# Attention written as a list of 260 operations that overlaps three batches, and the first output weights prepared during the experts

## The chip, the cores and the metric

The kernel runs on one core of one Trainium2 chip. The metric is the device time of one execution, in microseconds (us). Before the change three runs took 483.46, 483.88 and 485.32 us; the median is 483.88 us. The names of the engines are those of the profile: PE is TensorE, DVE is VectorE, ACT is ScalarE, POOL is GpSimd and SP is SyncE, which issues the transfers here.

## The reference, cut to what matters

Three layers follow each other: an attention between 512 tokens and 32 state rows of each head (8 batches, 8 heads, 64 columns), a soft mixture of 8 experts over all 4608 rows, and a gated layer over the same rows.

```python
scores = x @ state.T * scale;  a = softmax(scores);   xread = a @ state      # per batch and head
scores2 = state @ x.T * scale; a2 = softmax(scores2); sread = a2 @ x
x = concat([xread, sread])                            # rows: 8 * (512 + 32), 512 columns
logits = x @ phi                                      # 32 slots
d = softmax(logits, over all rows); slot_input = d.T @ x
slot_out[e] = relu(slot_input[e] @ w1[e]) @ w2[e]     # 8 experts, 4 slots each
y = softmax(logits, over slots) @ slot_out
g = y @ w_gate;  out = (g * sigmoid(g) * (y @ w_val)) @ w_out
```

## The kernel before

All instructions are recorded in the order of the Python text, and every engine works through its own part of that order, one instruction after the other. Nothing reorders them; an instruction that waits holds up everything behind it on its engine.

The attention takes one batch per turn of `for b in range(B - 1)`. A turn computes the scores of batch b (`scores`: PE matmuls into a PSUM bank pair, ACT copy into the one SBUF tile `stsA`), the largest score of each state row (`scores_max`, DVE), the shift of `stsA` by it (`state_shift`, DVE), transposes of the unshifted scores (`tr8`, PE) with the row maxima and the subtraction (`attn_sub`, DVE), the exponentials (`attn_exp`, ACT), the row sums and reciprocals (`attn_norm`, DVE) and the multiplication (POOL). In the same turn the state side is done (`state_tr`, `sread_mm`, `sread_out`), and the logits and slot sums of the two batches before (`attn_tr`, `logits_mm`, `logits_max`, `logits_exp`, `logits_tr`, `slots_mm`, `slots_out`). `load_T` makes the transposed x of batches 3 to 7 on PE. The last batch stands behind the loop, cut into two halves of 256 tokens, with `fill` matmuls that compute nothing used. Behind it come the 64 state rows' own logits (`sr_T`, `sr_mm`, `sr_exp`, `sr_tr`), the weights of the batches among each other (`mx`, `gm`, `w`, `Jw`), and the slot inputs `siT`.

Large PSUM tiles come from three bank pairs in turn (`pbig`), small ones from two banks in turn (`psmall`), so a PE group also waits for whoever reads the tile that had the bank before it.

All loads stand in one list and are issued by SP in that order (`pump`). A tile of the weight ring (17 tiles of 1 MB) or one of the borrowed attention tiles (`A`, `a2`, `e2`, `a0`, `at`) takes the next weights when the attention has finished with it.

The experts come in two groups of four: `expert_1` (w1), `expert_r` (relu), `expert_h` (transposes), `expert_2` (w2), `expert_o` (slot outputs to `ST`). Between them stand pieces of other work: the softmax over slots (`c_calc`), the first gate and value weights (`prep_w0`), and the first output weights. The output weights arrive as float64 bits and are rebuilt as float32 by `to32` (one ACT and three DVE instructions). Of the first 1 MB of them one half is loaded early and rebuilt by `prep_wo0`; the other half comes behind the last expert weights, and `wo0_load`, `wo0_shift`, `wo0_bits`, `wo0_scale`, `wo0_hi` and `wo0_lo` rebuild, scale and split it. Their instructions stand inside `expert_o(1)`, `prep_first` and the start of the main loop. `prep_first` goes from the slot outputs to the first gate and value weights; then the main loop (`front`, `middle`, `back`) runs over the rows.

Of the kernel before, what the change touches and what calls it, by code (L numbers as in the profile page):

```python
# [66 lines left out]
def attn_moe_glu_kernel(  # L67
# [152 lines left out]
    def load_T(b, half):  # L220
        if b >= B or b not in XT_PE:
            return
# [6 lines left out]
        p = pbig([128, 2, S])  # L229
        for kk in range(2):  # L230
            kc = 2 * half + kk
            for j in range(4):
                pe.transpose(p[:, kk, j * 128:(j + 1) * 128], x_[:, j, kc, 1:129], ident)
        (act.copy, XTE)[half](out=xT[b][:, 2 * half:2 * half + 2, :], in_=p)  # L234

    def score_mm(b, x_, p, cols):
        n = cols.stop - cols.start
        for pr in range(4):
            for hh in range(2):
                r = slice(64 * hh, 64 * hh + 64)  # L240
                pe.matmul(out=p[32 * pr:32 * pr + 32, hh, 0:n], lhsT=stB[r, b, pr, :], rhs=x_[r, pr, cols],
                          start=True, stop=True)

    def scores(b):
        x_ = xT.pop(b) if b in XT_PE else got.pop(("xt", b))
        p = pbig([128, 2, S])
        score_mm(b, x_, p, slice(0, S))
        done()
        t = stsA
        act.activation(out=t, in_=p, func=AF.Copy, scale=SCALE)  # L250
        sts[b] = t

    def scores_max(b):
        nm = sm.tile([128, 2], F32, tag="nm2", name="nm2")
        dve.tensor_reduce(out=nm, in_=sts[b], axis=AX.X, op=ALU.max, negate=True)  # L255
        RZ[b] = nm

    def state_shift(b):
        nm, t = RZ.pop(b), sts[b]
        for q in range(2):  # L260
            dve.tensor_scalar(out=t[:, q, :], in0=t[:, q, :], scalar1=nm[:, q:q + 1], scalar2=None, op0=ALU.add)  # L261

    def tr8(src):
        p = pbig([128, 4, 256])
        for j in range(4):
            for q in range(2):
                pe.transpose(p[:, j, q * 128:(q + 1) * 128], src[q][:, j * 128:(j + 1) * 128], ident)  # L267
        return p

    def attn_sub(b):  # L270
        t = sts[b]
        v = tr8([t[:, 0, :], t[:, 1, :]])
        state_shift(b)
        a = wk.tile([128, 4, 256], F32, tag=f"a{b % 3}", name="a")
        for i in range(2):
            vi, ai = (u[:, 2 * i:2 * i + 2, :].rearrange("p j (h s) -> p (j h) s", s=NS) for u in (v, a))
            m1 = sm.tile([128, 16], F32, tag="m1", name="m1")
            dve.tensor_reduce(out=m1, in_=vi, axis=AX.X, op=ALU.max)  # L278
            dve.tensor_tensor(out=ai, in0=vi, in1=bc(m1, NS), op=ALU.subtract)  # L279
        A[b] = a  # L280

    def attn_exp(b):
        a = A[b]
        for i in range(2):
            act.activation(out=a[:, 2 * i:2 * i + 2, :], in_=a[:, 2 * i:2 * i + 2, :], func=AF.Exp)  # L285

    def attn_norm(b):
        a = A[b]
        av = a.rearrange("p j (h s) -> p (j h) s", s=NS)
        z = sm.tile([128, 32], F32, tag="z", bufs=1, name="z")  # L290
        for i in range(2):
            dve.tensor_reduce(out=z[:, 16 * i:16 * i + 16], in_=av[:, 16 * i:16 * i + 16, :], axis=AX.X, op=ALU.add)
        dve.tensor_scalar(out=z, in0=z, scalar1=EPS, scalar2=None, op0=ALU.add)
        r = sm.tile([128, 32], F32, tag="r", bufs=1, name="r")
        dve.reciprocal(out=r, in_=z)
        pool.tensor_tensor(out=av, in0=av, in1=bc(r, NS), op=ALU.mult)  # L296
# [10 lines left out]

    def state_tr(b):
        t = sts[b]
        p = tr8([t[:, 0, :], t[:, 1, :]])  # L310
        e = wk.tile([128, 4, 256], F32, tag="e2", name="e2")
        act.activation(out=e, in_=p, func=AF.Exp)  # L312
        E2N[b] = e

    def sread_mm(b):
        x_, e = got.pop(("xn", b)), E2N.pop(b)
        p = psmall([128, 130])
        for q in range(2):
            for j in range(4):
                for c in range(4):  # L320
                    k = 128 * q + 32 * c
                    pe.matmul(out=p[32 * c:32 * c + 32, 65 * q:65 * q + 65], lhsT=e[:, j, k:k + 32],
                              rhs=x_[:, j, c, 65 * q:65 * q + 65],
                              start=(j == 0), stop=(j == 3))
        done()
# [1069 lines left out]
```

## Time and profile before

| | |
|---|---|
| median of the runs | 483.88 us |
| the profiled execution, its own time | 485.54 us |
| its span, first to last instruction | 483.80 us |
| PE busy | 450.9 us (93%) |
| DVE busy | 318.2 us (66%) |
| ACT busy | 253.1 us (52%) |
| POOL busy | 157.6 us (33%) |
| mean granted TensorE clock | 0.995 of full speed |

The stages, read from the timeline: start until the first scores at 8.95 us, attention until the first expert matmul at 101.28 us, experts until ACT copies the last w2 sums at 140.02 us, `prep_first` until the first output matmul at 150.21 us, and the main loop until 483.8 us. The shares in the table are means over these stages, and the main loop is 333.6 us of the 483.8, so they say little on the 150 us in front of it.

### The profile page before, as it was taken

How to read it: one execution, taken by the hardware profiler on the slowest of the kernel's cores; microseconds unless marked ns; L12 is line 12 of the kernel's file. 1: busy time of each engine (PE TensorE's matmuls, PEld its weight loads, DVE VectorE, ACT ScalarE, POOL GpSimd, SP SyncE). 2: the span in 40 equal slices, each digit the busy share in tenths (PEclk: the TensorE clock that was granted, in tenths of full speed). 3: DMA queues.
4: the chain of work that ended last, by engine and by line, in shares of the span. 5: the costliest groups of instructions: out<-in, count | busy, mean ns of one | idle time of the engine just before them, and what ended most of it. 6: DMA issues, size and time to landing. Idle time of an engine off the chain costs nothing.

```text
span 483.8 us, 9235 instructions
## 1 busy us (share of the span) xinstructions
PE 450.9 (93%) x3661; PEld 246.9 (51%) x3661; DVE 318.2 (66%) x643; ACT 253.1 (52%) x432; POOL 157.6 (33%) x134
## 2 busy tenths in 40 slices
PE   6688888999898999998999899999999999999995
PEld 5456665645354454454455454455555555555552
DVE  1888888657647868859989879867433343344454
ACT  1367766424418989676555455535444444444440
POOL 0111311127023333443443343334433333333331
PEclk9999999999899999999999999999999999999999
DMA  8999995869999920202000000000011112112124
GB/s 304 424 417 414 417 409 189 296 252 379 424 398 423 383 88 1 88 0 87 3 0 1 0 1 1 1 0 2 0 45 43 45 55 77 44 45 87 45 87 175
DMA packets 16219, 74.37 MB, mean 154 GB/s; under 512 B 1584, under 2 KB 2992, under 8 KB 9392
## 3 DMA queue, kind: packets, MB, share of 16 engines
q1 hardware_dynamic: 16176, 73.78, 38.9%
q8 instruction: 29, 0.48, 0.4%
q14 instruction: 14, 0.11, 0.1%
HBM read 64.87 MB, written 8.91 MB: 153 GB/s over the span
## 4 chain that ended last, share of the span: by engine, by line
PE 71%; DVE 15%; ACT 8%; issue 3%; DMA 1%; POOL 0%; SPq 0%; DVEq 0%; ACTq 0%; POOLq 0%
PE p L1279 49%; PE p L1245 8%; PE p L482 3%; PE p L513 3%; DVE a L279 2%; ACT xT L234 2%; DVE m L278 2%; DMA u<-in_xt_dram 1%; DVE atA L261 1%; DVE sh L1250 1%; DVE gvf L568 1%; PE s L733 1%; ACT e L312 1%; PE s L745 1%; PE p L267 1%
## 5 line engine op out<-in xcount | busy, mean ns | idle before, releaser
L1279 PE MATMUL p<-wo,hl 128*128 128x512 f16 x1020 | 235.0, 379 | 3.9 <-DVE osb L1290 3.3
L1259 POOL TENSOR_TENSOR hl<-sh,hl 128x512 f16<-128x512 f32 x102 | 126.1, 1237 | 201.0 <-ACT hl L1258 113.8
L1279 PEld LDWEIGHTS <-hl 128*128 128x128 f16 x1224 | 119.2, 98 | 129.2 <-issue 4.5
L1250 DVE SCALAR_TENSOR_TENSOR sh<-p,segk,sh 128x512 f32<-128x512 f32 x102 | 76.4, 749 | 94.1 <-ACT sh L1246 85.4
L1258 ACT CAST hl<-sh 128x512 f16<-128x512 f32 x102 | 62.9, 616 | 114.8 <-PE p L1279 80.9
L1246 ACT ACTIVATE sh<-p,sg 128x512 f32<-128x512 f32 x85 | 58.3, 686 | 5.7 <-PE p L1245 1.0
L1290 DVE SCALAR_TENSOR_TENSOR osb<-p,segm,osb 128x512 f32<-128x512 f32 x62 | 45.3, 746 | 10.9 <-PE p L1279 10.9
L1279 PE MATMUL p<-bqm,hl 128*128 128x512 f16 x204 | 46.8, 379 | 0.0
L1245 PE MATMUL p<-cstack,gvs 128*128 128x256 f16 x272 | 41.2, 273 | 2.4 <-DVE gvs L891 1.3
L1245 PEld LDWEIGHTS <-gvs 128*128 128x128 f16 x272 | 25.9, 98 | 20.5 <-issue 3.2
L296 POOL TENSOR_TENSOR a<-a,r 128x1024 f32<-128x1024 f32 x7 | 13.4, 1914 | 66.1 <-DVE md L365 48.3
L1245 PE MATMUL p<-cstack,gv 128*128 128x256 f16 x136 | 20.6, 273 | 0.9 <-DVE segm L806 0.9
L1288 ACT ACTIVATE osb<-p,segk 128x512 f32<-128x512 f32 x26 | 17.1, 687 | 3.3 <-PE p L1279 3.1
L568 DVE SCALAR_TENSOR_TENSOR gvf<-u,gvf 128x512 uint32<-128x512 uint32 (+1 forms) x22 | 18.6, 859 | 0.1
L1245 PEld LDWEIGHTS <-gv 128*128 128x128 f16 x136 | 13.0, 98 | 10.1 <-issue 1.7
L572 DVE SCALAR_TENSOR_TENSOR gvf<-u,gvf 128x512 uint32<-128x512 uint32 (+1 forms) x22 | 18.0, 840 | 0.1
L267 PE MATMUL p<-cs,atA 128*128 128x128 f32 x120 | 16.4, 277 | 1.2 <-DVE atA L261 1.0
L255 DVE TENSOR_REDUCE nm<-atA 128x2 f32<-128x1024 f32 x8 | 9.7, 1218 | 10.3 <-ACT atA L250 10.3
L267 PEld LDWEIGHTS p<-cs,atA 128*128 128x128 f32 x120 | 13.3, 141 | 4.2 <-DVE atA L261 2.4
L562 ACT ACTIVATE gvf<-u 128x512 f32<-128x512 f32 (+1 forms) x22 | 15.3, 716 | 0.0
L513 PE MATMUL p<-u,exq 128*32 128x256 f32 x256 | 14.6, 380 | 0.7 <-ACT exq L503 0.7
L285 ACT ACTIVATE a<-a 128x512 f32<-128x512 f32 x14 | 8.8, 631 | 11.2 <-DVE a L279 11.2
(254 smaller groups left out, 499.2 us busy)
## 6 DMA issues: line engine op xcount, KB each, us to landing
u<-in_w_dram SPq DMA_DIRECT2D x24, 1024.0 KB, 14.1
u<-in_wgv_dram SPq DMA_DIRECT2D x12, 1024.0 KB, 15.8
u<-in_xn_dram SPq DMA_DIRECT2D x8, 1040.0 KB, 18.4
out_dram<-osb SPq DMA_DIRECT2D x15, 512.0 KB, 2.8
early<-in_w_dram SPq DMA_DIRECT2D x12, 512.0 KB, 8.7
u<-in_wo_dram SPq DMA_DIRECT2D x5, 1024.0 KB, 12.7
u<-in_xt_dram SPq DMA_DIRECT2D x3, 1024.0 KB, 8.6
u<-in_wo_dram SPq DMA_DIRECT2D x2, 512.0 KB, 11.1
```

The source lines that it names most:

```text
L267: pe.transpose(p[:, j, q * 128:(q + 1) * 128], src[q][:, j * 128:(j + 1) * 128], ident)
L513: pe.matmul(out=SO[g][i][32 * j:32 * j + 32, :], lhsT=hT[g, k // 4][:, k % 4, 32 * j:32 * j + 32], rhs=u[:, j, :], start=(k == 0), stop=(k ...
L568: dve.scalar_tensor_tensor(out=tu[:, c], in0=lo[:, c], scalar=29, in1=tu[:, c], op0=ALU.logical_shift_right, op1=ALU.bitwise_or)
L572: dve.scalar_tensor_tensor(out=tu[:, c], in0=hi[:, c], scalar=0x80000000, in1=tu[:, c], op0=ALU.bitwise_and, op1=ALU.bitwise_or)
L1245: pe.matmul(out=p[v][:, 256 * i:256 * i + 256], lhsT=GV[2 * q + i][v], rhs=rhs, start=True, stop=True)
L1246: act.activation(out=sh[:, 0, :], in_=p[0], func=AF.Silu, scale=sgs[q])
L1250: dve.scalar_tensor_tensor(out=sh[:, 1, :], in0=p[1], scalar=(kap0[0] if k == 0 else seg_scale(*seg)[0][q]), in1=sh[:, 0, :], op0=ALU.mult ...
L1258: act.copy(out=t[:, 0, :], in_=sh[:, 1, :])
L1259: pool.tensor_tensor(out=t[:, 1, :], in0=sh[:, 1, :], in1=t[:, 0, :], op=ALU.subtract)
L1279: pe.matmul(out=accs[i], lhsT=t[:, u // 2, c], rhs=WO[2 * q + j][:, u % 2, :], start=first and u == 0 and j == 0, stop=last and (j, u) == ...
L1288: act.activation(out=o, in_=a, func=AF.Copy, scale=rsc)
L1290: dve.scalar_tensor_tensor(out=o, in0=a, scalar=rsc, in1=o, op0=ALU.mult, op1=ALU.add)
```

## The change

The functions of the attention become small operations `op_*`, each with the instructions of one engine, and a string lists the 260 calls. A name like `A0.4` is operation `A`, half 0, batch 4. Per batch: `SC` scores on PE, `SE` their copy on ACT, `NM` the maximum and `SH` the shift on DVE, `T80`/`T81` the transposes, `M0`/`M1` row maxima and `A0`/`A1` subtraction on DVE, `EX` exponentials on ACT, `Z` sums and `R` reciprocals on DVE, `N` the multiplication on POOL, `ST`, `E2`, `SR`, `SO`, `SRC` the state side, `AT`, `ATc`, `LG`, `LC`, `MD`, `LE`, `LT`, `ED`, `LGc`, `SL`, `QS` logits and slots, `Xt`/`Xc` the transposed x. Behind the batches: `Rt` to `Rs` the state rows' logits, `P`, `mask`, `mx`, `pm`, `gm`, `w`, `wd`, `Jw`, `Q`, `Qt`, `pPs`, `S`, `si` down to the slot inputs. The `fill` matmuls of the last batch are gone. The borrowed tiles are given to the loader by `ready`, when the named operations are recorded. Three lines of the list show its kind, the first and two from the middle and the end.

```diff
+ORDER = """
+B1 Bc SPm SC.0 SPc SE.0 T80.0 NM.0 T81.0 SH.0 M1.0 ST.0 M0.0 SC.1 E2.0 A0.0 A1.0 SE.1 SR.0 EX0.0 NM.1 T80.1
...
+T81.7 M0.7 AT.5 A0.7 Rt.0 ATc.5 M1.7 A1.7 Rc.0 LG.5 NM.7 Rm.0 LC.5 EX0.7 AT.6 Rl.0 SH.7 EX1.7 ATc.6 MD.5 ST.7
...
+SL.6 ED.7 LGc.7 Rd.1 P.0 mx Re.1 QS.6 Rr.1 pm1 Rs.1 gm P.1 w wd SL.7 pPs Jw QS.7 S0 Q.0 Q.1 Qt.0 S1 Qt.1 S2
+si0 si1
+"""
...
-            push(("wo", 0, 0), wo[0, :, 0:512], I64)
+            push(("wo", 0), wo[0], I64)
...
-    push(("wo", 0, 1), wo[0, :, 512:1024], I64)
...
+    def bank(key, shape, big=True):
+        val[key] = (pbig if big else psmall)(shape)
+        return val[key]
...
+    def op_SC(b):
+        score_mm(b, bank(("s", b), [128, 2, S]), slice(0, S))
+        x_left(b)
+        if b == 0:
+            heat(HB)
+
+    def op_SE(b):
+        act.activation(out=stsA, in_=val.pop(("s", b)), func=AF.Copy, scale=SCALE)
...
+    def op_T8(i, b):
+        if ("v", b) not in val:
+            bank(("v", b), [128, 4, 256])
+        s_tr(val["v", b], (2 * i, 2 * i + 1))
...
+    def op_A(i, b):
+        if ("a", b) not in val:
+            val["a", b] = wk.tile([128, 4, 256], F32, tag=f"a{b % 3}", name="a")
+        dve.tensor_tensor(out=halves(("a", b), i), in0=halves(("v", b), i), in1=bc(val.pop(("m", i, b)), NS), op=ALU.subtract)
...
+    def op_Nh(i, b):
+        v = halves(("a", b), i)
+        (pool, dve)[i].tensor_tensor(out=v, in0=v, in1=bc(val["r", b][:, 16 * i:16 * i + 16], NS), op=ALU.mult)
...
-        if i:
+        if i and not g:
             dve.tensor_scalar(out=h, in0=p, scalar1=rd, scalar2=0.0, op0=ALU.mult, op1=ALU.max)
         else:
             act.activation(out=h, in_=p, func=AF.Relu, scale=rd)
...
-        (act.copy, dve.tensor_copy)[i](out=t, in_=q)
+        (act.copy, dve.tensor_copy)[i and not g](out=t, in_=q)
...
     def prep_wo0():
         t = wk.tile([128, 1024], F32, tag="gvf", bufs=4, name="wof")
...
+        yield from to32(("wo", 0), t)
+        mx = sm.tile([128, 1], F32, tag="mxw", bufs=1, name="mxw")
+        dve.tensor_reduce(out=mx, in_=t, axis=AX.X, op=ALU.max, apply_absolute_value=True)
+        Q, R = yield from scale_bits(mx, 1, "wo")
+        sc = sm.tile([128, 1], F32, tag="wsc", bufs=1, name="wsc")
+        dve.tensor_scalar(out=sc, in0=R, scalar1=2.0 ** 14, scalar2=None, op0=ALU.mult)
+        w = wk.tile([128, 2, 1024], F16, tag="at", bufs=1, name="wo16")
+        for i in range(2):
+            c = slice(512 * i, 512 * i + 512)
+            act.activation(out=w[:, 0, c], in_=t[:, c], func=AF.Copy, scale=sc)
         yield 1
+        for i in range(2):
+            c = slice(512 * i, 512 * i + 512)
+            dve.scalar_tensor_tensor(out=w[:, 1, c], in0=t[:, c], scalar=sc, in1=w[:, 0, c], op0=ALU.mult, op1=ALU.subtract)
+            WO[i] = w[:, :, c]
...
+        def ready(seen):
+            for tag, need in (("A", {"SC0.7", "SC1.7", "T80.7", "T81.7", "SH.7", "ST.7"}), ("a2", {"SL.5", "AT.5"}),
+                              ("e2", {"SR.7"}), ("a0", {"SL.6", "AT.6"}), ("at", {"LG0.7", "LG1.7"})):
+                if tag in late and need <= seen:
+                    free(tag)
+
+        seen = set()
+        for name in ORDER.split():
+            op, _, b = name.partition(".")
+            OPS[op](*([int(b)] if b else []))
+            seen.add(name)
+            ready(seen)
...
-        some(pg, G0)
-        run(c1)
+        some(pg, 10)
         expert_1(1, 0, 1)
-        some(pg, G2)
-        run(c2)
-        expert_1(1, 1, 2)
-        run(c3)
-        some(pw, 4)
         expert_o(0)
         warm = sm.tile([128, 1], F32, tag="warm", bufs=1, name="warm")
         act.activation(out=warm, in_=va, func=AF.Silu)
+        run(c1)
+        expert_1(1, 1, 2)
+        run(c2)
         expert_1(1, 2, 4)
         expert_r(1, 0)
-        some(pg, 11 - G0 - G2)
-        expert_1(1, 4, G1)
-        run(pw, pg)
-        expert_1(1, G1, 7)
+        run(c3)
+        some(pg, 1)
+        expert_1(1, 4, 5)
+        run(pg)
+        some(pw, 1)
+        expert_1(1, 5, 7)
         expert_h(1, 0)
         room[1] = 9
         expert_1(1, 7, 8)
         expert_r(1, 1)
+        some(pw, 4)
         expert_2(1, 0, 3)
         expert_h(1, 1)
-        for u in range(3, 8):
-            expert_2(1, u, u + 1)
-            if 3 < u < 7:
-                heat(H2, 0)
+        expert_2(1, 3, 4)
+        run(pw)
+        expert_2(1, 4, 8)
         expert_o(1)
...
-        wo0_shift()
-        wsc = wo0_scale(gvp[1][1][:, 0:128])
...
-            if v:
-                wo0_hi(0)
```

The first place is DVE in one middle turn of the attention. In the kernel before, the turn of batch 4 begins like this: `nm` is the maximum of the scores, `z` and `r` with 128x2 and `srC` the state side of batch 3, `edn` the slot weights of batch 2, `atA` the shift, `m` and `a` row maxima and subtraction, `z` with 128x16 and 128x32 the sums of batch 4.

```order
L255 TENSOR_REDUCE nm_741<-atA 128x2
L331 TENSOR_SCALAR z_776<-s_743 128x2
L333 RECIPROCAL r_778<-z_776 128x2
L338 TENSOR_TENSOR srC<-s_743,r_778 32x128 x4
L383 COPY edn<-s_784 128x128
L261 TENSOR_SCALAR atA<-atA,nm_741 128x512 x2
L278 TENSOR_REDUCE m_802<-p_790 128x16
L279 TENSOR_TENSOR a<-p_790,m_802 128x512
L278 TENSOR_REDUCE m_805<-p_790 128x16
L279 TENSOR_TENSOR a<-p_790,m_805 128x512
L292 TENSOR_REDUCE z<-a 128x16 x2
L293 TENSOR_SCALAR z<-z 128x32
```

In the changed kernel the same turn begins like this; `edn` belongs to batch 1, and the sum `z` with its reciprocal `r` to batch 3.

```order
L298 TENSOR_REDUCE nm_742<-atA 128x2
L306 TENSOR_SCALAR atA<-atA,nm_742 128x512 x2
L323 TENSOR_REDUCE m_765<-p_744 128x16
L323 TENSOR_REDUCE m_778<-p_744 128x16
L430 COPY edn<-s_780 128x128
L343 TENSOR_REDUCE z<-a 128x16
L347 TENSOR_SCALAR z<-z 128x32
L349 RECIPROCAL r<-z 128x32
L328 TENSOR_TENSOR a<-p_744,m_778 128x512
L328 TENSOR_TENSOR a<-p_744,m_765 128x512
L372 TENSOR_SCALAR z_847<-s_809 128x2
L374 RECIPROCAL r_849<-z_847 128x2
```

The shift has moved up to directly behind the maximum, the two subtractions have moved down behind the sum and reciprocal of the batch before, and the state side stands behind them.

The second place is the start of PE's queue, up to the first transposes of scores. In the kernel before: `stN` are the state rows of batches 0 to 3 and then of 4 to 7, `atA` with `u` the first scores, `atA` with `phs` the products of state rows and phi (64 matmuls), and `ones` and `cs` alone are matmuls whose results nobody reads.

```order
L302 MATMUL p_139<-ones 128x128 x7
L399 MATMUL p_147<-cs,stN 128x128 x4
L302 MATMUL p_153<-cs 128x128 x5
L241 MATMUL p_159<-u,atA 32x512 x8
L302 MATMUL p_173<-cs 128x128 x5
L399 MATMUL p_179<-cs,stN 128x128 x4
L267 MATMUL p_185<-cs,atA 128x128 x8
L267 MATMUL p_205<-cs,atA 128x128 x8
L1005 MATMUL p_223<-phs,atA 32x32 x64
```

In the changed kernel:

```order
L587 MATMUL p_139<-ones 128x128 x7
L447 MATMUL p_147<-cs,stN 128x128 x4
L587 MATMUL p_153<-cs 128x128 x5
L447 MATMUL p_159<-cs,stN 128x128 x4
L458 MATMUL p_165<-phs,atA 32x32 x64
L253 MATMUL p_230<-u,atA 32x512 x8
L587 MATMUL p_241<-cs 128x128 x5
L311 MATMUL p_249<-cs,atA 128x128 x8
L311 MATMUL p_264<-cs,atA 128x128 x8
```

The second state rows and the products with phi now stand in front of the first scores.

The third place is DVE at the start of `prep_first`, behind the last slot outputs `ST`. In the kernel before, `wof`, `mxw` and `wP` are the first output weights, `P`, `Q` and the 128x4 and 128x2 scalars the scales of the slot outputs, `mw` the gate and value weights:

```order
L546 TENSOR_TENSOR ST<-s_1956,ST 128x128
L846 TENSOR_REDUCE mst<-ST 128x1
L676 TENSOR_TENSOR mxw<-mxw 128x1
L678 TENSOR_SCALAR wof<-wof 128x512
L685 SCALAR_TENSOR_TENSOR wof<-u,wof 128x256
L599 TENSOR_REDUCE P<-s_1997 128x1
L604 TENSOR_SCALAR Q<-P 128x1
L608 RECIPROCAL R<-Q 128x1
L866 TENSOR_SCALAR s_2016<-sc,R 128x4
L867 TENSOR_SCALAR s_2016<-sc,Q 128x2
L697 TENSOR_REDUCE wP<-p_1982 128x1
L699 TENSOR_SCALAR wP<-wP 128x1
```

In the changed kernel, from the last instruction of the output weights (`wo`) on:

```order
L831 SCALAR_TENSOR_TENSOR wo_1914<-wof,wsc,wo_1914 128x512 x2
L688 COPY so<-p_1864 128x256
L704 TENSOR_TENSOR ST<-s_1956,ST 128x128
L957 TENSOR_REDUCE mst<-ST 128x1
L757 TENSOR_REDUCE P<-s_1991 128x1
L762 TENSOR_SCALAR Q<-P 128x1
L766 RECIPROCAL R<-Q 128x1
L974 TENSOR_SCALAR s_2008<-sc,R 128x4
L975 TENSOR_SCALAR s_2008<-sc,Q 128x2
L983 TENSOR_REDUCE mw<-p_2011 128x2
```

All work on the output weights now stands in front of the slot outputs, and only the scales of the slot outputs and weights are left behind them.

## Rows read from the trace of the kernel before

**Rows 1.** Stretches: us; PE, PEld, DVE, ACT, POOL busy (instructions); clock; DMA share; GB/s

```profile
11.19:19.45 8.26, 5.48 (x169) 3.71 (x167) 7.00 (x12) 3.57 (x5) 0.87 (x1) 1.00 1.01 423
11.19:86.39 75.20, 61.87 (x1153) 45.68 (x1152) 64.00 (x138) 46.66 (x83) 13.40 (x7) 1.00 0.92 375
39.29:49.13 9.84, 8.53 (x148) 6.26 (x146) 8.40 (x19) 7.00 (x13) 1.88 (x2) 1.00 1.01 408
86.39:101.28 14.89, 14.09 (x230) 9.78 (x228) 8.41 (x33) 6.92 (x20) 1.46 (x1) 1.00 0.81 284
122.00:124.00 2.00, 0.86 (x8) 0.87 (x8) 1.93 (x3) 1.35 (x4) 0.00 (x0) 1.00 1.02 430
124.00:128.00 4.00, 4.00 (x22) 1.13 (x25) 3.21 (x6) 1.95 (x4) 0.00 (x0) 0.57 1.02 426
132.43:140.02 7.59, 7.59 (x136) 4.34 (x132) 1.44 (x2) 0.00 (x0) 0.00 (x0) 1.00 1.05 391
```

**Rows 2.** Waits of DVE from 29.35 to 69.31: total us, times, longest

```profile
DVE nm L255 <- ACT atA L250: 2.8, 4, 0.8
DVE atA L261 <- PE p L267: 0.5, 3, 0.2
```

**Rows 3.** Waits of PE from 9 to 101.3

```profile
PE p L241 <- DVE a L279: 1.8, 3, 0.6
```

**Rows 4.** Timeline of the start: start us, us, engine, line, operation

```profile
3.06 0.69 SPq L957 DMA_DIRECT2D stN<-in_stn_dram  x1
8.95 1.09 PE L241 MATMUL p<-u,atA 64*32 64x512 f32 x16 [2.58 <-DMA u<-in_xt_dram]
10.13 1.02 ACT L250 ACTIVATE atA<-p 128x1024 f32<-128x1024 f32 x1 [8.12 <-PE p L241]
11.19 1.22 DVE L255 TENSOR_REDUCE nm<-atA 128x2 f32<-128x1024 f32 x1 [5.21 <-ACT atA L250]
11.21 0.66 PE L399 MATMUL p<-cs,stN 128*128 128x128 f32 x4
12.33 0.68 DVE L400 COPY atA<-p 128x512 f32<-128x512 f32 x1
14.77 1.29 PE L1005 MATMUL p<-phs,atA 64*32 64x32 f32 x128
```

**Rows 5.** Transfers issued from 3.0 to 3.5: KB each, us from issue to landing

```profile
stN<-in_stn_dram SPq DMA_DIRECT2D x1, 256.0 KB, 6.9
```

**Rows 6.** Timeline of the last batch, behind its reciprocals

```profile
86.56 1.46 POOL L1052 TENSOR_TENSOR a<-a,r 128x512 f32<-128x512 f32 x1 [6.24 <-DVE r L1050]
88.08 1.09 PE L1058 MATMUL p<-cs,a 128*128 128x128 f32 x8 [0.31 <-POOL a L1052]
98.97 0.91 DVE L1156 STREAM_TRANSPOSE QT<-s 128x256 f32<-128x256 f32 x2 [1.58 <-PE s L1153]
99.85 1.12 PE L1163 MATMUL p<-QT,stN 128*64 128x32 f32 x32
```

**Rows 7.** Timeline of the experts

```profile
121.03 2.76 SPq L156 DMA_DIRECT2D u<-in_w_dram  x1
123.14 1.08 PE L531 MATMUL s<-cs,so 128*128 128x32 f32 x8 [1.29 <-ACT so L529]
124.14 4.48 PE L482 MATMUL p<-u,siT 128*32 128x512 f32 x24
129.19 1.92 PE L482 MATMUL p<-u,siT 128*32 128x512 f32 x16
135.81 4.52 PE L513 MATMUL p<-u,exq 128*32 128x256 f32 x80
```

**Rows 8.** Transfers issued from 120.95 to 121.5

```profile
u<-in_w_dram SPq DMA_DIRECT2D x1, 512.0 KB, 17.9
```

**Rows 9.** Timeline of `prep_first`

```profile
146.50 0.41 DVE L685 SCALAR_TENSOR_TENSOR wof<-u,wof 128x256 uint32<-128x256 uint32 x1
147.29 0.46 DVE L604 TENSOR_SCALAR Q<-P 128x2 uint32<-128x2 uint32 x1
```

More of the change, by code (lines that the diff above doesn't have):

```diff
@@ L228, in load_T @@
                 room[1] = 0
-        p = pbig([128, 2, S])
+        p = bank(("x", half, b), [128, 2, S])
         for kk in range(2):
-            kc = 2 * half + kk
             for j in range(4):
[L233 to L237, printed above, removed]
-        for pr in range(4):
[L239 to L274, printed above, removed]
-        for i in range(2):
[L276 to L296, printed above, removed]
+                pe.transpose(p[:, kk, j * 128:(j + 1) * 128], x_[:, j, 2 * half + kk, 1:129], ident)
@@ new lines, in op_ATch, with l_mm @@
+    def op_ATch(i, b):
+        if ("at", b) not in val:
+            val["at", b] = wk.tile([128, 2, S], F32, tag="at", bufs=1, name="at")
+        act.copy(out=val["at", b][:, :, 256 * i:256 * i + 256], in_=val.pop(("ah", i)))
+    def l_mm(b, js):
+        if ("l", b) not in val:
+            bank(("l", b), [128, 128], False)
+        for q in range(2):
+            for j in js:
+                pe.matmul(out=val["l", b][32 * j:32 * j + 32, :], lhsT=SP[:, b, q, :],
+                          rhs=val["at", b][:, q, j * 128:(j + 1) * 128], start=(q == 0), stop=(q == 1))
@@ new lines, in op_ED, with op_LGc, op_SL @@
+    def op_ED(b):
+        val["ed", b] = wk.tile([128, 128], F32, tag="edn", bufs=2, name="edn")
+        (act.copy if EDA else dve.tensor_copy)(out=val["ed", b], in_=val["lt", b][:, 1, :])
+    def op_LGc(b):
+        act.copy(out=Lg[:, 2 + 4 * b:6 + 4 * b, :], in_=val["lt", b][:, 0, :].rearrange("p (j s) -> p j s", s=NSL))
+    def op_SL(b):
+        e, a = val.pop(("ed", b)), val.pop(("a", b))
+        p = bank(("q", b), [128, 256], False)
+        for j in range(4):
+            pe.matmul(out=p[32 * j:32 * j + 32, :], lhsT=e[:, 32 * j:32 * j + 32], rhs=a[:, j, :], start=True, stop=True)
@@ new lines, in op_wd, with op_Q @@
+    def op_wd():
+        wd = sm.tile([128, 9], F32, tag="wd", bufs=1, name="wd")
+        dve.tensor_tensor(out=wd, in0=val["w"], in1=ds, op=ALU.mult)
+        val["wds"] = sm.tile([128, 1], F32, tag="wds", bufs=1, name="wds")
+        dve.tensor_reduce(out=val["wds"], in_=wd, axis=AX.X, op=ALU.add)
+    def op_Q(g):
+        p = bank(("pq", g), [128, 256], False)
+        for i in range(4):
+            pe.matmul(out=p[32 * i:32 * i + 32, :], lhsT=val["Jw"][:, 4 * g + i, :], rhs=QS[:, 4 * g + i, :],
+                      start=True, stop=True)
@@ L306, in fill @@
             pe.matmul(out=hz, lhsT=ident, rhs=ident, start=True, stop=True)
[L308 to L325, printed above, removed]
-        P4[b] = p
```

581 lines of the change are left out of this document (230 added, 351 removed).

## The prediction

> **What bounds the kernel now.** I read the busy slices first, then the stretches, the waits and the timeline of each stage. The main loop holds PE all but full, and its code is the same apart from a few instructions at its start, so all that can move lies in the first 150 us. There each stage has its own limit.
>
> In the attention no engine is full. In a middle turn of 9.84 us DVE works 8.40, PE 8.53 and ACT 7.00 [rows 1]. DVE waits 1.44 us per turn. By name that is about 0.8 for the copied scores and 0.2 for the transposes [rows 2]; the other 0.44 are the short gaps between its instructions. PE in turn waits for DVE's subtraction before it can take the bank for the next scores, 0.6 us in a turn [rows 3]. So it is a ring: scores, copy, maximum, shift, subtraction, next scores, which no engine leaves for long. From the first maximum at 11.19 to the last reciprocal's end at 86.39 DVE works 64.0 of 75.2 us [rows 1, 4]. Behind that is a chain with one thing after the other: 14.89 us, in which DVE works 8.41 and PE 14.09, part of it fills [rows 1].
>
> The experts look like PE's stage, and PE loses time in them: it waits 1.29 us for a copy on ACT at 123.14 and then runs from 124 to 128 at a mean granted clock of 0.57, so mostly at the lower level, 1.2 GHz [rows 1, 7]. But the DMA is full there too (share 1.02, 426 GB/s). The last half tile of w2 is issued at 121.03 and takes 17.9 us to land, so it is there at 138.93 [rows 7, 8]. PE uses it for the last 8 of the 80 records before 140.02, about 0.43 us of work, so from about 139.6 on. No wait shows, but only 0.65 us are to spare.
>
> `prep_first` is a chain of small DVE steps from 140.02 to the first output matmul at 150.21.
>
> **The change, part by part. The start.** The state rows of batches 4 to 7 and the products with phi now stand in front of the first scores on PE. These state rows are issued at 3.06 and land 6.9 us later, at 9.96 [rows 4, 5]. From there: transposes 0.66, DVE copy 0.68, the second half of the products 0.65, scores 1.09, copy 1.02, and five hops of about 0.05: the first maximum starts at 14.3 instead of 11.19, 3.1 later [rows 4]. The cover that it loses is the wait for x, which ended at 8.95. It gets the 1.29 us of products off PE later, where they cost nothing either.
>
> **The turns.** From the first maximum to the last reciprocal DVE has the same instructions, less the copy of the second state rows (0.68, now ahead of it), and with the state side of batch 6 (1.5), one logits maximum (0.3) and the copies of the first state rows' logits (0.4), which stood behind it: 64.0 - 0.68 + 2.2 = 65.5 us. What it waits I lay by hand from the new order. The short gaps stay: 0.44 for each of seven turns, 3.1. Behind the first subtraction it waits 0.6 for the second scores, since shift, transposes, scores and copy are longer than what it has. At batch 2 it waits 0.4 behind the transposes of x for batch 3, which PE does first. At batch 4 the shift stands straight behind the maximum, and the transposes that must read the scores before it end 0.6 too late. At batch 7 the logits of batch 5 and the state rows' logits come through ACT 1.1 late. In the other turns the ring closes: from the subtraction's end to the next maximum PE and ACT need 1.09 + 1.02 + hops = 2.4 us, and DVE has 2.5 us of state side, logits maximum and sum standing there. Sum of waits 3.1 + 0.6 + 0.4 + 0.6 + 1.1 = 5.8, so the last reciprocal ends at 14.3 + 65.5 + 5.8 = 85.6, 0.8 before 86.39. The bounds are no wait at all (79.8) and the wait of today, 11.2 (91.0). I take 5.8, since the two waits that have a name today are the two that the new order fills.
>
> **The tail.** Today it is 14.89. In the new order nothing of other batches stands in batch 7's way, and no fill does. The chain by the durations of the same operations in this stretch [rows 6]: POOL's half of the multiplication 1.46, its transposes 0.55, copy 0.58, logits 0.64, copy, maximum and exponential 0.97, transposes 0.38, copy 0.29, eight hops of 0.07: 5.45 to the slot weights of batch 7. Then the state rows' second half holds the weights of the batches: maxima 0.44, exponential 0.40, transposes and broadcast 0.51, `gm` 0.29, `w` 0.30, `wd` 0.32, `Jw` 0.46, first third of the sums 0.55, `Q` 0.8, the two `Qt` 0.91, last third 0.55, `si` 0.22, and 0.7 of hops: 6.45. That is 11.9, with the last hop to the first expert 12.0. Bounds: 12.0 and 14.9; I take 12.0, as each step is in the trace. The attention then ends at 97.6, 3.7 before 101.28.
>
> **The experts.** All their releases of the weight ring are tied to their own instructions, so the stream of weights moves with the attention's end, and the load that is made whole (1 MB instead of 0.5) fits into the time when the DMA is idle: its share in the tail is 0.81 [rows 1]. `expert_o(0)` moves in front of the copies on ACT that held it, and I lay PE at the second w2 about 2.1 us earlier, with the slow clock gone. But the last half tile lands at 138.93 less the attention's 3.7, and PE needs it 0.65 later today. So 0.6 is what this stage gives; the other 1.5 become a new wait for weights. DVE's new work on the output weights is 0.7 + 3 x 1.2 + about 1.0 + 1.5 us; DVE works only 1.44 of the last 7.59 us of this stage [rows 1], so there is room for it. Bounds: 0 and 0.65.
>
> **`prep_first`.** Between the slot outputs and the first output matmul DVE loses 12 instructions of the output weights. Most stand beside waits for PE. What the chain gives is the step at 146.50 (0.41) in front of the scale's maximum, and most of the 0.46 us of the next one, two columns that took so long beside POOL's work on the same weights [rows 9]: 0.7 in all. Bounds 0.3 and 1.5.
>
> The sum goes against the profiled execution: 485.54 - 3.7 - 0.6 - 0.7 = 480.5. The median of the runs, 483.88, is 1.66 lower than that execution, so the forecast is 483.88 - 5.0 = 478.9.
>
> **The rivals. The clock falls in the tail.** The tail loses its fills, and in my layout PE idles 3.0 of 12 us. The rows for it: with 0.86 busy of 2.0 us PE lost its clock, and 24 records took 4.48 us where 16 take 1.92 [rows 1, 7]. Against it: in the first 8.3 us of the attention PE was busy 5.48 (66%) at a full clock of 2.4 GHz [rows 1], and 75% is more. If it falls, the 3.9 us of PE steps in the tail's second half take 1.6 to 2 times as long: 2.3 to 3.9 more, say 3.1. That gives 482.0. The Trainium skill, in "TensorE: Matmul & The Clock Gate", section "What's actually happening", states that the clock is gated by how busy PE has lately been and that the slow state is the default; by that rule a tail without fills is where it would fall, and the trace agrees with it at 124 us, though not on what share is enough.
>
> **DVE hardly waits.** If the new order closes the ring in every turn, only the 3.1 of short gaps stay: the reciprocal ends at 82.9, the attention at 94.9, 6.4 earlier; with 1.3 behind it 476.2. For it speaks that DVE needs 8.4 us a turn and the others no more; against it, that PE with 8.53 has as little room.
>
> **Slower: the ring gets longer.** The subtraction now stands behind copy, sum and reciprocal of other batches, and the next scores wait for it [rows 3]. Maximum 1.2, shift 0.9, row maxima 1.4, those three 1.5, subtractions 1.4, scores 1.1, copy 1.0 and hops make 9.1. If in addition the state-side matmuls stand in front of the scores on PE, or the exponentials in front of the copy on ACT, 1.1 to 1.8 us that I laid beside DVE's work, a turn takes 10.6 instead of 9.84. Six turns lose 4.6, and the 3.1 of the start is lost in full; tail and later stages give 4.2 back, so 3.5 is lost: 487.4. It decides from about 10 us a turn; the layout has 9.1 to 9.3.
>
> **How the numbers follow.** Forecast 0.54, DVE hardly waits 0.20, clock 0.17, longer ring 0.09. A measurement of this kernel can tell some 0.5%, 2.4 us, from no change: faster is below 481.5, slower above 486.3. The forecast's own bounds (waits 4 to 9, tail 12.0 to 13.5) leave 0.03 of its 0.54 above 481.5; of the clock's case a third is faster; of the longer ring's 0.03 stays within. Faster 0.51 + 0.20 + 0.06 = 0.77, same 0.03 + 0.11 + 0.03 = 0.17, slower 0.06. The range from 475.8 to 482.6 takes in the case with few waits and most of the clock's, and leaves out the longer ring.
>
> **What would show it.** Right: the first maximum near 14.3; some 9.2 us between maxima of batches 3 to 6, with DVE's wait for the copy of the scores nearly gone; the first expert matmul near 97.6; a wait of PE for a w2 tile of about 1 us just before the last one; 9.5 us from the last w2 to the first output matmul. Wrong: a granted clock under 1.00 between 85 and 98, turns of 9.8 and more, PE never waiting for weights, or a main loop that is not 333.6 us long.

## The result, and the profile after

The change takes 1.2% off the time: 478.43 us (478.4 to 479.22, four runs) against 484.47 us of the kernel before beside it; ratio 0.988, 95% interval 0.9855 to 0.9905. A second measurement later on, beside other kernels, gave 478.27 against 483.77 us, 0.9894 (0.9875 to 0.9913). Forecast were 478.9 us.

The profiled execution took 479.22 us with a span of 477.4, 6.4 us shorter than the span before. I cut it at the same rows in both traces: the first maximum, the end of the last reciprocal, the first expert matmul, DVE's copy of the last sums of the experts (before 140.47, after 135.60), the first output matmul.

| us | before | after | difference |
|---|---|---|---|
| start to first maximum | 11.19 | 12.62 | +1.43 |
| first maximum to end of last reciprocal | 75.20 | 72.24 | -2.96 |
| tail to first expert matmul | 14.89 | 12.37 | -2.52 |
| experts to copy of the last sums | 39.19 | 38.37 | -0.82 |
| from there to the first output matmul | 9.74 | 9.03 | -0.71 |
| main loop | 333.59 | 332.77 | -0.82 |

Not all of this is the change. In the profiled execution of the kernel before the state rows took 6.9 us to land [rows 5]; in the other thirteen profiles they took 5.2 to 5.7. With the old attention and loads that land sooner (wo_only, below) the first maximum starts at 9.08 and the first expert matmul at 100.17, so against that profile the attention gains 2.9 to 4.0 us (its end is 97.23 here and 96.19 in a second profile of the same kernel), where the first three rows add up to 4.05. And the 0.82 of the main loop stands behind the last instruction of DVE, here before and after:

```profile
478.67 0.75 DVE L1290 SCALAR_TENSOR_TENSOR osb<-p,segm,osb 128x512 f32<-128x512 f32 x1 [0.55 <-PE p L1279]
473.69 0.75 DVE L1208 SCALAR_TENSOR_TENSOR osb<-p,segm,osb 128x512 f32<-128x512 f32 x1 [0.54 <-PE p L1197]
```

From the first output matmul to there the main loop is 0.60 us longer after the change (329.06 against 328.46). From there to the end of the span it is 5.13 us before and 3.71 after; all other profiles have 3.65 to 3.84.

The medians also hold the falls of the clock. Of 57 executions of the kernel before beside the experiments, the 24 with a mean clock of 0.995 or 0.996 took 481.82 to 483.77 us, the 17 with 0.991 or less 483.41 to 486.33. The nine of the kernel after have 0.996 to 1.000 and took 477.78 to 479.22.

The stretches of the profile after, in the columns of [rows 1]; the first and the fifth answer to the second and fourth row there, the second to fourth are the turns of batches 3 to 5:

```profile
12.62:84.86 72.24, 61.28 (x1044) 44.19 (x1047) 63.81 (x146) 48.67 (x86) 13.41 (x7) 0.98 0.97 393
36.12:47.53 11.41, 10.38 (x232) 7.89 (x231) 10.28 (x27) 8.30 (x16) 1.83 (x1) 1.00 1.01 414
47.53:56.42 8.89, 7.91 (x146) 6.02 (x144) 8.31 (x20) 6.40 (x11) 2.00 (x2) 1.00 1.03 416
56.42:65.67 9.25, 8.70 (x153) 6.75 (x151) 8.01 (x21) 7.82 (x15) 1.92 (x1) 1.00 1.01 416
84.86:97.23 12.37, 11.67 (x194) 7.45 (x183) 6.10 (x22) 5.74 (x18) 1.46 (x1) 1.00 0.78 309
...
30.00:32.00 2.00, 0.90 (x5) 0.74 (x6) 1.94 (x6) 1.32 (x2) 0.00 (x0) 0.89 1.01 420
32.00:34.00 2.00, 2.00 (x21) 0.85 (x19) 1.87 (x6) 0.88 (x1) 0.00 (x0) 0.50 1.04 428
34.00:36.00 2.00, 2.00 (x26) 1.16 (x11) 1.36 (x6) 1.08 (x2) 1.91 (x1) 0.75 0.99 410
```

The reader is to see three things. DVE's work is nearly that of before (63.81 against 64.00 us) in a stretch 3 us shorter. The tail, without its fills, kept the full clock; PE works 11.67 of its 12.37 us, where the prediction laid 3.0 of 12 us idle. And the clock did fall elsewhere, from 31 to 35.5 us, to a mean of 0.50 in one slice: a place that no step of the prediction names.

The timeline of the start and of that place (start us, us, engine, line, operation, the wait before it):

```profile
8.43 0.63 PE L447 MATMUL p<-cs,stN 128*128 128x128 f32 x4 [2.34 <-DMA stN<-in_stn_dram]
...
24.96 1.94 PE L273 MATMUL p<-cs,u 128*128 128x128 f32 x16 [0.88 <-DMA u<-in_xn_dram]
26.74 1.04 PE L311 MATMUL p<-cs,atA 128*128 128x128 f32 x8
28.10 1.09 PE L387 MATMUL p<-cs,a 128*128 128x128 f32 x8 [0.32 <-POOL a L353]
31.09 1.93 PE L311 MATMUL p<-cs,atA 128*128 128x128 f32 x8 [1.90 <-DVE atA L306]
32.95 1.96 PE L253 MATMUL p<-xT,atA 64*32 64x512 f32 x16
```

The state rows of batches 4 to 7 are there at 8.4, not at 9.96 as [rows 5] gave it. At 24.96 PE waits for x of batch 3, which stands before the transposes of batch 2 in its order, then 1.90 us for the shift of batch 2, and what follows runs at half the clock (L311 1.93 us where the L311 row at 26.74 has 1.04). DVE pays for it here:

```profile
27.81 0.69 DVE L323 TENSOR_REDUCE m<-p 128x16 f32<-128x512 f32 x1 [1.29 <-PE p L311]
...
36.12 1.22 DVE L298 TENSOR_REDUCE nm<-atA 128x2 f32<-128x1024 f32 x1 [0.66 <-ACT atA L285]
37.77 0.69 DVE L323 TENSOR_REDUCE m<-p 128x16 f32<-128x512 f32 x1 [0.42 <-PE p L311]
```

Behind 36.12 no maximum waits for the copied scores any more, where [rows 2] had 2.8 us in four turns. In the experts PE is now up to 0.43 us ahead of the weights; before, none of these waits showed. The row, and the transfer that it waits for (117 us, its time to landing):

```profile
134.90 0.64 PE L672 MATMUL p<-u,exq 128*32 128x256 f32 x8 [0.43 <-DMA u<-in_w_dram]
```

```profile
116.98 17.87 DMA u<-in_w_dram
```

It lands at 134.85, 4.08 us earlier than before [rows 8], as much as the attention's end moved (4.05).

### The profile page after: what moved, and what is told of

It is laid out like the page before. It is cut to its first block, busy times and chain, and to the rows that moved or that the text cites. A ratio compares the mean times of both kernels' runs of the same rounds, so it can differ in the third digit from the quotient of the medians.

```text
span 477.4 us, 9171 instructions
## 1 busy us (share of the span) xinstructions
PE 448.6 (94%) x3637; PEld 243.9 (51%) x3637; DVE 316.4 (66%) x633; ACT 256.0 (54%) x434; POOL 153.7 (32%) x131
## 4 chain that ended last, share of the span: by engine, by line
PE 72%; DVE 12%; DMA 8%; ACT 4%; issue 2%; POOL 0%; SPq 0%; DVEq 0%; ACTq 0%
PE p L1197 49%; PE p L1163 8%; DMA u<-in_w_dram 4%; DMA u<-in_xn_dram 4%; PE p L311 2%; PE p L641 2%; PE p L672 2%; PE p L273 2%; DVE a L328 2%; DVE sh L1168 1%; DVE gvf L726 1%; PE s L844 1%; DVE m L323 1%; PE p L253 1%; DMA cs<-in_cst_dram 1%
## 5 line engine op out<-in xcount | busy, mean ns | idle before, releaser
L311 PE MATMUL p<-cs,atA 128*128 128x128 f32 x128 | 19.1, 285 | 5.3 <-DVE atA L306 4.3
L311 PEld LDWEIGHTS p<-cs,atA 128*128 128x128 f32 x128 | 14.6, 144 | 8.3 <-DVE atA L306 2.2
L723 DVE TENSOR_SCALAR gvf<-gvf 128x512 uint32<-128x512 uint32 (+1 forms) x22 | 12.1, 566 | 2.2 <-ACT gvf L720 1.9
```

Of the source, the lines that this page charges most:

```text
L311: pe.transpose(p[:, j, q * 128:(q + 1) * 128], stsA[:, q, j * 128:(j + 1) * 128], ident)
```

## The experiments

Twelve runs were made, four at a time; each four share a chip and the runs of the kernel before. Two of them repeat a kernel. "Stretch" is the time from the first maximum to the end of the last reciprocal, 72.24 us in the profile after.

**The two parts alone (before 483.13 us).** The list of operations (it has 322 names; the 260 ahead of the prediction is a miscount) goes into the kernel before, with the old lines for the output weights kept; and the other way round.

```diff
 attn_only: ORDER and its operations new; these lines as before
+            push(("wo", 0, 0), wo[0, :, 0:512], I64)
...
+        wo0_shift()
+        wsc = wo0_scale(gvp[1][1][:, 0:128])
 wo_only: the old attention; prep_wo0, expert_r, expert_h and the order of the experts new
```

> The new list of operations for the attention with the old treatment of the first output weights (two half transfers, shift and bits behind the experts). Theory, the two parts add: attention ends near 97.2 us as in the kernel after (101.28 before), the experts, the stretch from the last w2 to the first output matmul and the main loop keep the times of before (38.7, 10.2 and 333.6 us), so 484.5 - 4.05 = 480.4 us, ratio 0.9916. Rival, weights bind: the w2 transfers do not come 4 us sooner, the experts' end moves by only 2 to 3 us, 481.5 to 482.5 us, and PE waits for DMA before the last w2 matmuls.

Measured: 480.74 us, ratio 0.9935 (0.991 to 0.9959). The attention ends at 97.18, as in the kernel after (97.23), and the experts take 39.21 us; so far the theory. PE shows no wait for a w2 tile, which the rival wanted. But the stretch behind them takes 10.72 us instead of 9.74, and the stretches say why:

```profile
120.00:125.00 5.00, 5.00 (x30) 1.57 (x29) 3.11 (x6) 2.44 (x4) 0.00 (x0) 0.66 1.01 419
143.00:145.00 2.00, 0.93 (x5) 0.56 (x6) 1.60 (x7) 1.51 (x3) 0.70 (x1) 0.83 0.99 414
145.00:147.00 2.00, 2.00 (x11) 1.69 (x10) 1.97 (x6) 1.20 (x2) 0.51 (x1) 0.50 1.03 430
147.00:149.00 2.00, 2.00 (x10) 0.91 (x9) 1.46 (x3) 1.21 (x2) 1.51 (x2) 0.82 0.99 410
```

The old wait in the experts still costs the clock near 121 us, as in [rows 1], and the many small DVE steps of the old output weights leave PE 0.93 busy of 2 us at 143, after which it falls again. In the profile before the same steps left PE 0.91 busy of 2 us from 147 to 149 at a clock of 1.00, so they do not cost it in every execution. Of its twelve executions the two with a mean clock of 0.999 took 478.10 and 478.56 us, as long as the whole change takes; the four with 0.988 took 481.49 to 482.18.

> The old attention with the new treatment of the first output weights and the new interleaving in the experts. Theory: attention end 101.3 us as before; experts 0.4 us shorter, last w2 to first output matmul 9.1 instead of 10.2 us, main loop 332.8 instead of 333.6 us because the rest of the weights' splitting no longer stands in its first blocks: 484.5 - 2.35 = 482.1 us, ratio 0.9951. Rival: the main loop's 0.8 us belongs to the new attention (transfers that start earlier), so 482.9 us. Rival 2: with the attention late the weights are no limit, so the experts gain about 1 us: 481.6 us.

Measured: 481.77 us, ratio 0.9973 (0.9949 to 0.9996), between the theory's 482.1 and rival 2's 481.6. Experts 38.37 and the stretch behind them 9.03 us are to the digit those of the kernel after, with the same wait of 0.4 us for w2, though the attention ends 3 us later; so rival 2 falls by its mechanism. The attention, which was to end at 101.3 as before, ends at 100.17. The main loop is 332.23 us here and 332.59 in attn_only, both shorter than the 333.59 before, and with an end of 3.76 and 3.84 us behind DVE's last instruction. So neither theory nor rival has the cause of the 0.82: it is the end of that one profiled execution, 5.13 us, and why it was so long is open. The two ratios multiply to 0.9908, the whole has 0.988 and 0.9894; the rest is within the intervals.

**The dip at 31 us (dip_fill and dip_order beside the two above; dip_fill6 and order_fill in a second group, before 483.51 us).** First the clock alone, with 12 and then 6 matmuls in the gap that compute nothing used; then another order, without and with such matmuls.

```diff
 dip_fill, dip_fill6 (F: the matmuls)
-... M1.2 AT.0 EX0.2 A1.2 ATc.0 SH.2 ...
+... M1.2 AT.0 F EX0.2 A1.2 ATc.0 SH.2 ...
 dip_order (order_fill: F behind Xt1.3, SO.1 before SRC.1)
-NM.2 Xt0.3 Xt1.3 SO.1 Xc0.3 R.0 Z1.1 T80.2 N.0 Xc1.3 T81.2 M0.2 A0.2 M1.2 AT.0 EX0.2 A1.2 ATc.0 SH.2 EX1.2 SRC.1 ST.2 SC.3 Z0.1 E2.2
+NM.2 T80.2 T81.2 SH.2 Xt0.3 Xt1.3 Xc0.3 SO.1 R.0 N.0 M0.2 Xc1.3 A0.2 EX0.2 M1.2 A1.2 EX1.2 ST.2 AT.0 E2.2 ATc.0 Z1.1 SC.3 SRC.1 Z0.1
```

> The kernel after with 12 matmuls of 128x128 that compute nothing used, between the transpose of batch 0 and the state transposes of batch 2, where PE stood idle for 1.90 us at 29.2 to 31.1 us. Theory, the clock costs time: the granted clock stays 1.00 from 30 to 36 us, state transposes 1.05 instead of 1.93 us, scores of batch 3 1.09 instead of 1.96 us; DVE's wait of 0.66 us for the scores of batch 3 and of 0.42 us behind it go, the attention ends 1.1 us earlier, 477.4 us. Rival, the loss lies behind DVE: DVE meets the next operand later instead, attention end within 0.3 us of 97.23, total within 0.3 us of the kernel after (478.4 us).

Measured: 480.31 us, ratio 0.9947 (0.9922 to 0.9971). The clock stayed at 1.00, but I had mis-sized the edit: each of these matmuls leaves two records, so 12 took 2.84 us and made the state side of batch 1 (`srC`), whose PSUM tile they write into, wait 1.48 us on DVE. The run says only that the clock can be held.

> As dip_fill, with 6 instead of 12 matmuls (12 of them took 2.84 us there, longer than the gap of 1.90 us, and held the state transposes until 33.06 us and the sums of batch 1 on DVE for 1.48 us); 6 take 1.42 us. Theory, the clock at half cost the 0.66 and 0.42 us that DVE waits at batch 3: clock 1.00 from 30 to 36 us, from the first maximum to the end of the last reciprocal 71.2 us instead of 72.24 us (kernel after), ratio to before about 0.986. Rival, off the critical path: that stretch stays 71.9 to 72.3 us and what is gained at batch 3 comes back as a wait further on.

Measured: 478.05 us, ratio 0.9887 (0.9865 to 0.9908). Clock 1.00, second to third turn 10.67 instead of 12.10 us, stretch 70.70 us, a little better than the theory's 71.2. But not by the clock alone: the first maximum came at 14.05 in this execution, so x of batch 3 was there in time and DVE waits 0.37 where it waited 1.29:

```profile
28.61 0.69 DVE L323 TENSOR_REDUCE m<-p 128x16 f32<-128x512 f32 x1 [0.37 <-PE p L311]
```

What the dip itself costs is the 0.66 and 0.42 us of waits, some 1.1 us where it comes. The total does not show it against 478.43, and the repeat of the kernel after (below) says why.

> The kernel after with the list changed in the turn of batch 2 only: both transposes and the shift of batch 2 directly behind its maximum, the transposes of x of batch 3, which wait for their transfer until 24.8 us, behind them, the state transposes before the transpose of batch 0. Theory, the wait for x of batch 3 and the late shift cost DVE's 1.29 us, the 0.66 us and the dip of the clock: batch 3's maximum starts near 34.0 instead of 36.12 us, the attention ends 1.5 to 2.2 us earlier, 476.2 to 476.9 us. Rival, a later turn takes it back (PE or ACT late by the time that DVE gains): batch 3's maximum is early, but the last reciprocal still ends within 0.5 us of 84.86 us, total 478.0 to 478.5 us.

Measured: 478.75 us, ratio 0.9896 (0.9862 to 0.9929), stretch 71.61 us. The theory fails: batch 3's maximum comes at 35.83, not 34.0. The last reciprocal ends where the rival has it (84.51), but the gain is lost in the same turn, not in a later one. PE got its work earlier and then had nothing for 2.82 us, so the clock fell in the same place, and DVE's wait for the scores of batch 3 grew from 0.66 to 1.26 us:

```profile
30.02 1.12 PE L311 MATMUL p<-cs,atA 128*128 128x128 f32 x8 [2.82 <-DVE a L328]
30.92 1.91 PE L387 MATMUL p<-cs,a 128*128 128x128 f32 x8
32.77 1.82 PE L253 MATMUL p<-xT,atA 64*32 64x512 f32 x16
```

> dip_order (transposes and shift of batch 2 first, x of batch 3 behind them) with 10 matmuls of 128x128 whose result is not used, 2.4 us, in the gap of 2.82 us in which PE waits there for DVE's subtraction; the sums of batch 1 stand a little later on DVE so that they do not wait for them. Theory: in dip_order the half clock at 30 to 36 us made the scores of batch 3 late, DVE waited 1.26 and 0.34 us for them; with the clock at 1.00 both waits go: second to third maximum (batch 2 to 3) 10.3 us instead of 11.5 us, first maximum to last reciprocal 70.2 us (dip_order 71.61, after 72.24), total 1.5 to 2 us below the kernel after. Rival: a later wait takes it, that stretch stays above 71.3 us.

Measured: 477.85 us, ratio 0.9876 (0.9858 to 0.9894). The stretch is 70.28 us and the turn 10.30, as expected, and the attention ends at 95.26. Of these 2 us the experts give 0.61 back: they take 38.98 us, and PE's wait for the last w2 grows to 0.8:

```profile
PE p L676 <- DMA u<-in_w_dram: 0.8, 1, 0.8
```

**How much the weights bind (second group).**

```diff
 w2_short
-        push(("w2", 1, 7, i), w2[1, 7, :, :, 256 * i:256 * i + 256])
+        if i == 0:
+            push(("w2", 1, 7, i), w2[1, 7, :, :, 256 * i:256 * i + 256])
```

> The kernel after without its last transfer of w2: the last eight matmuls of the experts read the half tile before it again, so half a tile of 512 KB is left out. Theory, the end of the experts is bound by the arrival of the weights: PE's wait before the last eight matmuls (0.43 us) goes, and the experts (first matmul to the last copy of the sums, 38.37 us) take 37.3 to 37.9 us, because the transfers behind it come 1.1 us sooner as well. Rival, PE is the bound, and the wait is the only thing that the transfers cost: 37.9 to 38.0 us. Rival 2: a wait for DVE or ACT takes its place: 38.3 us.

Measured: 478.04 us, ratio 0.9877 (0.9855 to 0.99). PE no longer waits for w2, and the experts take 37.73 us, 0.64 less: in the theory's range, but not for its reason. Up to the last eight matmuls PE's rows lie at the same times behind the first expert matmul, within 0.01 us, so nothing came sooner. Here the last 64 records run on without a stop:

```profile
130.33 3.66 PE L673 MATMUL p<-u,exq 128*32 128x256 f32 x64
```

In the kernel after 56 of them take 3.23 us, then come the wait of 0.43 and the last eight, which take 0.64 behind a stop and 0.43 here. So the last half tile of w2 is the bound at the end of this stage, and it costs 0.64 us.

**The start (start_early in the second group; the others in a third, before 483.77 us).**

```diff
 start_early
-B1 Bc SPm SC.0 SPc SE.0 T80.0 NM.0 T81.0 SH.0 M1.0 ST.0 M0.0 SC.1 E2.0 A0.0 A1.0 SE.1 SR.0 EX0.0 NM.1 T80.1 EX1.0 T81.1
+SC.0 SE.0 T80.0 NM.0 T81.0 B1 SH.0 M1.0 ST.0 M0.0 SC.1 E2.0 A0.0 A1.0 Bc SE.1 SR.0 EX0.0 NM.1 T80.1 EX1.0 T81.1 SPm SPc
 start_late
+            if op == "B1":
+                heat(HB, 2)
```

> The kernel after with the second half of the state (transposes, copy) and the slot products behind the first scores, as in the kernel before. Theory, transfers gate the first turns: the first maximum starts at 9 to 11.2 us instead of 12.6 us, but x of batch 3 still lands near 24.8 us, and PE, which waits 0.88 us for it, waits 2 to 3 us; the last reciprocal ends at 84.5 to 85 us, total within 0.5 us of the kernel after. Rival, the start counts in full: last reciprocal at 83.0 to 83.4 us, total 476.5 to 477.2 us, ratio 0.985 or less.

Measured: 482.51 us, ratio 0.9973 (0.9953 to 0.9994): 4 us slower than the kernel after. The first maximum comes at 9.34, 3.28 us earlier, but the third at 24.80, 0.78 later, and the last reciprocal ends at 85.78, 0.92 later. That is the profile of one of the shortest executions (480.44); the twelve have mean clocks from 0.996 down to 0.984, and the rest of the 4 us is not shown in it. The theory had a loss right, but its size (within 0.5 us of the kernel after) and its cause wrong: x of batch 3 is not waited for. PE stands three times for nothing that the trace names ("issue"):

```profile
14.18 1.93 PE L253 MATMUL p<-u,atA 64*32 64x512 f32 x16 [1.58 <-issue]
...
20.13 0.81 PE L458 MATMUL p<-phs,atA 64*32 64x32 f32 x70 [0.54 <-issue]
...
26.29 0.66 PE L366 MATMUL s<-u,e 128*32 128x65 f32 x32 [2.10 <-issue]
```

That is 4.22 us, and the way from the first to the third maximum is 15.46 instead of 11.40 us, 4.06 more. The kernel before has two such waits:

```profile
20.25 1.10 PE L322 MATMUL s<-u,e 128*32 128x65 f32 x61 [1.88 <-issue]
...
26.76 1.09 PE L241 MATMUL p<-u,atA 64*32 64x512 f32 x16 [1.26 <-issue]
```

wo_only, with the same old start, has two of 1.97 and 1.17 us, ending at 18.23 and 25.59. The kernels with the products in front have none between 8 and 40 us in any of their ten profiles.

> order_fill with the early start of start_early. Theory, transfers gate the first turns: first maximum near 9.3 us, last reciprocal not before 82.9 us (order_fill), total at or above order_fill. Rival, what start_early lost was only the wait for x of batch 3 in front of the transposes of batch 2, which stand first here: last reciprocal 80 to 82 us, total 1 us or more below order_fill.

Measured: 480.22 us, ratio 0.994 (0.9921 to 0.9959). First maximum 9.23, last reciprocal 85.33, PE's nameless waits 2.1, 1.6 and 1.1 us. The theory's side, with the same other cause; the rival falls.

> The kernel after with five matmuls of 128x128 that compute nothing used (about 1.3 us) behind the transposes of the second half of the state, so that the first scores and the first maximum come about 1 us later. Theory, transfers gate the first turns and an early start costs the clock: first maximum near 13.7 us, no or less wait for x of batch 3, clock 1.00 at 30 to 36 us, last reciprocal at 84.0 to 84.9 us, total not above the kernel after. Rival, the start counts in full: last reciprocal at 86 us, total 1 to 1.3 us above it.

Measured: 480.15 us, ratio 0.9938 (0.9919 to 0.9958), 1.9 us above the kernel after beside it. The profiled execution was the shortest of its six (479.07): first maximum 14.75, clock 1.00, stretch 70.27, end of the last reciprocal 85.02. In this profile the theory's dip-free stretch came, and the last reciprocal ends 1 us before the rival's 86; in the total the rival is nearer, with 1.9 us against its 1 to 1.3. A later start costs time here, but the first maximum differs between executions too (12.60 to 14.05 in profiles of the unchanged start), and how much of the 1.9 us is the start is open.

**The kernel after once more, and order_fill beside it.**

> The kernel after, unchanged, beside the three below. Both theories: 478.4 us, ratio 0.985 to 0.991. If the dip of the clock hangs on how early the first maximum starts, executions with a mean clock of 1.00 are about 1 us shorter than those with 0.996.

> The same kernel as order_fill, beside the kernel after on the same chip. Theory: attention ends 2 us earlier than in the kernel after, the experts take 0.6 us longer because the last w2 lands only 1.2 to 1.4 us earlier: 0.8 to 1.4 us below the kernel after. Rival, the difference of order_fill was chance: within 0.3 us of the kernel after.

Measured: 478.27 us for the kernel after, 478.45 us, ratio 0.9898 (0.9879 to 0.9918), for order_fill. The rival is right: order_fill is no better in the total. The kernel after's executions with a mean clock of 0.999 or 1.000 took 477.78 to 478.44 us, those with 0.996 478.05 to 479.22: 0.4 us apart in the mean, not 1 us. In this profile of the kernel after the dip did not come, though PE was as little busy as in the first, 1.09 and 0.94 of 2 us (1.09 and 0.90 there; its gap in front of the state transposes is 1.48 us here and was 1.90):

```profile
28.00:30.00 2.00, 1.09 (x8) 0.85 (x8) 1.93 (x4) 0.78 (x2) 0.43 (x1) 1.00 0.95 399
30.00:32.00 2.00, 0.94 (x7) 0.78 (x8) 1.94 (x6) 1.28 (x2) 0.00 (x0) 1.00 1.05 437
32.00:34.00 2.00, 2.00 (x26) 0.99 (x24) 1.87 (x6) 1.51 (x2) 0.03 (x1) 1.00 1.01 416
```

Its stretch is 70.80 us, the third turn 11.04 instead of 12.10. So order_fill has 0.4 to 0.5 us on it. In its first profile the experts take that back (38.98 against 38.43 us here), in the second (38.33) the start was 0.94 us later. No experiment gave a kernel faster than the change itself by more than its runs differ.

## Why the prediction was right, step by step

**The bound (a ring that no engine leaves for long): right.** DVE's work stayed, its named wait for copied scores in the middle turns went, and the turns of batches 4 and 5 take 8.89 and 9.25 us where 9.2 were laid. The turn of batch 3 has 11.41 (11.02 without the dip) with more of the other batches' work in it (DVE 10.28): one of the three turns forecast at 9.2, and past the 9.8 that was named as a sign of being wrong.

**The start, +3.1: the shift right, its base and its effect wrong.** The chain was right: 4.34 us from the landing of the state rows to the first maximum. Where the loads land alike the shift is as laid (3.28 between start_early and the kernel after). But they landed 1.7 us earlier than in the profile before, which was the latest of all, so the maximum came at 12.62 instead of 14.3. What the step missed is that the products in front are worth more than they cost: with the old start (start_early) PE stands 4.2 us for nothing named, and the kernel before has 3.14 us of it, which I had read in no row.

**The turns, 65.5 us of work and 5.8 of waits: the end right, the terms not.** Work 63.81, 1.7 less than laid, the rest 8.43, 2.6 more. The laid waits behind batch 0, at batch 2 and at batch 7 are there (0.75, 1.29 and 0.75 us); the 0.6 at batch 4 is not. Not laid were the transfer of x of batch 3, which makes 1.29 out of 0.4, the dip of the clock behind it, 1.08 us of waits, and a wait of 0.61 for ACT's copy of the logits in the turn of batch 5. The end of the last reciprocal, 84.86 against 85.6 forecast, comes out of a start 1.7 too late and a stretch 0.9 too short: errors that cancel, and so luck.

**The tail, 12.0: right** (12.37), with the clock at 1.00. The rival in which the clock falls there did not happen, and was not put to the test: PE idles 0.70 us, not 3.0. Its mechanism was real but 50 us further up, where PE waits for a transfer and then for DVE. The Trainium skill, in "TensorE: Matmul & The Clock Gate", section "What's actually happening", says that the clock follows how busy PE has lately been. The traces agree (attn_only at 143 us, dip_order at 30 us). The two profiles of the kernel after, one with the dip and one without at nearly the same busy times, show that one program can go either way.

**The experts, -0.6, bound by the last w2: right, the size past its bound** (-0.82 where 0.65 was the most, with a wait of 0.43 us where 1 us was laid). The stage was cut at ACT's copy at 140.02, but the 80 records of w2 end at 140.33 [rows 7] and DVE copies the last sums at 140.47, so there was more to spare than 0.65. wo_only has the same gain with the attention as before, w2_short takes the wait away, order_fill lengthens it.

**`prep_first`, -0.7: right** (-0.71). The step of 0.41 is gone, and the one of 0.46 [rows 9] takes 0.17 now:

```profile
142.00 0.17 DVE L762 TENSOR_SCALAR Q<-P 128x2 uint32<-128x2 uint32 x1
```

That the change can also take away a second dip, which attn_only shows at 143 us, was not seen. **The main loop, unchanged: not quite.** Its work is 0.60 us longer, and the 0.82 less is the late end of the profiled execution before.

The rivals with a longer ring and with hardly any waits did not happen: DVE still stands 8.43 us, and the turns of batches 4 and 5 take 9 us.

The forecast of 5.0 us less stands against 6.04 and 5.50 in the two measurements. It is close in part by luck: it was worked out from an execution whose first loads and whose end were late, and of the falls of the clock that the medians of the kernel before hold it has only the one at 124 us.

## What to carry to other kernels

A new order is worth what its slowest hand-over in each stage leaves: here the attention gave 2.9 to 4.0 us, and in order_fill 0.6 of a further gain went to a stream of weights that had only 0.65 us to spare. When work is moved to the front, look at what the engine would have waited for anyway, also at waits that the profile gives no name to. And a gap on PE can cost twice, once as a wait and once as half a clock behind it. Before a difference between two profiles is put down to a change, look whether other executions of the same code show it: here the start and the end of one profile made some 2.5 us.
